# Reordered first quarter, undivided score visits and 13 constant products in an attention and MLP kernel

## Chip, cores and metric

One core of one Trainium2 chip runs the kernel. The metric is device time in microseconds (us). A smaller number is better.

## What is computed

Eight batches of eight heads, 576 queries of 64 elements, with 16 beacon keys ahead of the 576 ordinary ones; then a two-layer MLP over all 4608 tokens:

```python
scores = scale * np.matmul(q, k_all.transpose(0, 1, 3, 2))   # k_all = [beacon_k, k]
scores = np.where(causal, -1000000000.0, scores)              # beacons are always visible
a = np.exp(scores - scores.max(-1, keepdims=True))
a /= a.sum(-1, keepdims=True) + 1e-09
x = np.matmul(a, v_all)          # to [4608 tokens, 512]
h = x @ w_in                     # 512 -> 2048
out = (h * (1.0 / (1.0 + np.exp(-1.702 * h)))) @ w_out        # 2048 -> 512
```

## The kernel before

**Tiles.** A *set* is four heads of one batch, stacked on the 128 partitions, so a batch is two sets (0 and 1 for the first batch, 2 and 3 for the second). Loads of q and k (288 KB each) come through GpSimd's DMA queue, which also converts them to 16 bit. VectorE turns them (`e_turn`, L472) into `qT` and `kT`; a set can be scored once both are turned. The scores of a set are computed in *visits* (the program's chunks, `e_qk`, L509): 512 or 384 columns at a time for four heads, each followed by an exponential on ScalarE (L521) and masks on GpSimd or VectorE. Visits 0 to 15 belong to sets 0 to 3, four to a set; visits 8 to 11 are those of set 2 and visits 12 to 15 those of set 3. A visit is a list of pieces, one for each block of 128 keys; each piece is 2 products for each of 4 heads. `qk_pieces` sorts the pieces by width and, where the last one is wider than 64 columns, cuts 32 columns off it as a piece of its own: the narrow product.

**Values and MLP.** `av s.x.h` (L598) multiplies the exponentials of set s with the values: x = 2 gives the sums, x = 0 and 1 the two halves of the head; h is the half of the queries. Value blocks j = 0 to 4 and the beacon values are loaded separately. `av0.0.1` therefore needs blocks 3 and 4 of the first batch too. `e_norm` (L632) normalises into `xT`. `m1.g.n` (L656) is the first MLP product of token group g (groups 0 and 1 are 256 tokens, later ones 512) for columns n and n+1 of blocks of 128; `tanh` (ScalarE, L671) and `gate` (VectorE, L690) follow. `m2.g.mt.qt` (L702) is the second product for quarter qt of the rows of w2. Every `av`, `m1` and `m2` result stands in one of four PSUM banks (`RING`), which comes free when its norm, gate or eviction has run.

**Order.** `ORDER` gives, by hand, the order of work on every engine; its numbers count the calls of `plan.op`. The planner walks these lists with estimated durations, which decides PSUM banks and how many constant products are put into gaps. Each engine runs its list strictly in order. `Q` is the order in which the planner takes GpSimd's loads to be served, at most 8 of them in flight (`LANES`): load n is issued when load n-8 has landed. GpSimd also makes masks, so a mask listed behind a load waits for that load's turn. SyncE's list holds the beacon-key loads and the stores.

**Constant products.** TensorE has nothing to do until the first keys are turned. The loop at L1380 fills this and later gaps (until 20 us of the planned time) with products of a constant tile, `scrap`, written by VectorE at L327. A gap of n units of 256 columns gets n//4 products in 32 bit and n%4 in 16 bit.

Important names of the diff, in the order's numbering: TensorE 120, 138, 141 are visits 5, 6, 7; 236, 241, 243, 246 visits 8 to 11; 267, 272, 274, 277 visits 12 to 15; 409, 412, 415, 422, 440 visits 16 to 20. GpSimd 49 and 51 are the loads of k and q of set 2, 53 and 55 those of set 3; 25 and 27, 33 and 35, 37 and 39, 41 and 43 are the four column quarters of w1; 17, 19, 21, 23, 29, 31 the beacon values and value blocks 0, 1, 2, 3, 4 of the first batch; 45, 47, 57, 59 are w2; 16 builds the two mask tables. VectorE 235 and 234 turn q and k of set 2, 266 and 265 those of set 3.

Of the kernel before, what the change touches and what calls it, by code (L numbers as in the profile page):

```python
# [14 lines left out]

ORDER = {
    "PE": [
        76, 97, 99, 104, 106, 124, 111, 113, 127, 129, 116, 118, 145, 148, 150, 159, 120, 163, 160, 164, 138, 170,
        131, 141, 167, 173, 176, 236, 136, 152, 134, 157, 179, 241, 155, 182, 197, 243, 200, 203, 206, 246, 209, 212,
        267, 191, 221, 192, 185, 272, 215, 222, 274, 186, 218, 277, 187, 223, 193, 409, 224, 188, 194, 250, 255, 257,  # L20
        281, 253, 412, 227, 228, 229, 415, 288, 286, 262, 260, 291, 284, 293, 422, 230, 321, 311, 313, 309, 299, 303,
        317, 307, 319, 301, 305, 315, 329, 325, 327, 323, 440, 431, 347, 352, 353, 348, 349, 354, 350, 443, 434, 438,
        436, 355, 358, 469, 374, 359, 360, 368, 361, 575, 369, 363, 370, 375, 364, 578, 479, 365, 371, 376, 366, 584,
        482, 377, 484, 486, 603, 380, 516, 494, 605, 381, 382, 383, 518, 608, 488, 510, 514, 490, 498, 492, 504, 500,
        512, 508, 502, 506, 496, 547, 541, 542, 536, 537, 538, 543, 539, 594, 736, 548, 563, 544, 549, 550, 739, 564,
        565, 566, 599, 742, 617, 597, 601, 552, 553, 749, 624, 622, 554, 555, 620, 767, 557, 558, 559, 560, 626, 770,
        758, 569, 570, 571, 646, 572, 656, 636, 654, 796, 763, 761, 652, 644, 630, 632, 640, 638, 642, 628, 648, 634,
# [17 lines left out]
        1546, 1554, 1555, 1556, 1557, 1560, 1561, 1562, 1563,  # L45
    ],
    "ACT": [
        3, 1, 77, 78, 98, 100, 105, 107, 112, 114, 117, 119, 121, 161, 139, 165, 142, 168, 171, 174, 237, 177, 242,
        180, 183, 198, 244, 201, 204, 247, 207, 210, 268, 213, 273, 216, 275, 278, 219, 410, 189, 225, 195, 413, 416,
        424, 423, 231, 322, 312, 314, 300, 310, 318, 304, 308, 320, 306, 316, 302, 330, 326, 328, 324, 441, 351, 444,  # L50
        470, 471, 576, 579, 585, 586, 604, 606, 517, 519, 511, 489, 495, 515, 491, 493, 499, 513, 509, 501, 505, 503,
        507, 497, 609, 540, 737, 740, 743, 751, 750, 768, 771, 627, 647, 657, 637, 655, 797, 653, 633, 631, 639, 641,
        643, 645, 649, 629, 635, 651, 798, 903, 678, 906, 913, 912, 931, 933, 936, 838, 820, 826, 836, 816, 822, 832,
        834, 818, 846, 840, 824, 828, 830, 842, 844, 1064, 867, 1067, 1070, 1077, 1078, 1095, 1098, 1125, 1124, 960,
# [5 lines left out]
        1480, 1476, 1458, 1486, 1484, 1482, 1496, 1460, 1494, 1500, 1502, 1506, 1490, 1510, 1492, 1498, 1508, 1531,  # L60
    ],
    "DVE": [
        73, 75, 74, 101, 103, 102, 79, 87, 82, 80, 81, 125, 109, 110, 126, 108, 130, 128, 146, 147, 151, 149, 162,
        235, 132, 133, 166, 233, 234, 172, 175, 169, 137, 153, 154, 158, 135, 264, 178, 156, 265, 181, 419, 199, 184,
        92, 202, 266, 205, 406, 211, 208, 214, 408, 217, 407, 420, 220, 295, 251, 252, 256, 254, 258, 421, 259, 282,
        466, 283, 289, 287, 263, 261, 290, 285, 292, 294, 467, 468, 296, 427, 297, 428, 429, 335, 336, 298, 339, 581,
        331, 332, 430, 340, 341, 333, 343, 432, 342, 337, 433, 334, 338, 344, 345, 435, 439, 437, 356, 346, 475, 583,
        476, 477, 478, 362, 582, 480, 481, 733, 367, 746, 483, 372, 485, 487, 378, 384, 748, 747, 735, 734, 613, 590,
        520, 521, 591, 532, 533, 534, 592, 793, 528, 524, 535, 529, 525, 526, 530, 593, 527, 531, 595, 596, 522, 523,
        545, 551, 614, 615, 616, 600, 618, 598, 619, 602, 625, 754, 623, 621, 755, 556, 756, 757, 561, 908, 567, 794,  # L70
        759, 795, 760, 573, 764, 762, 802, 910, 803, 909, 1073, 804, 805, 658, 659, 670, 666, 766, 807, 667, 660,
# [12 lines left out]
        1526, 1542, 1547, 1552, 1558, 1564,  # L84
    ],
    "POOL": [
        10, 8, 14, 12, 17, 16, 25, 21, 19, 23, 35, 27, 49, 33, 51, 31, 37, 115, 39, 43, 29, 41, 53, 122, 123, 65, 63,
        140, 61, 45, 144, 55, 143, 67, 388, 47, 239, 386, 390, 69, 238, 57, 59, 245, 240, 249, 392, 400, 404, 269,
        271, 248, 71, 446, 270, 448, 276, 402, 394, 279, 398, 450, 280, 452, 411, 715, 414, 464, 713, 460, 719, 458,
        717, 417, 418, 456, 396, 425, 462, 442, 426, 445, 473, 472, 577, 775, 589, 727, 721, 729, 731, 588, 773, 474,  # L90
        580, 725, 607, 454, 1042, 587, 1040, 723, 777, 779, 611, 610, 738, 612, 741, 744, 745, 753, 789, 781, 752,
        772, 1044, 787, 783, 785, 1046, 769, 791, 800, 799, 1100, 1102, 904, 1050, 1056, 801, 1058, 907, 1048, 914,
        1054, 915, 934, 938, 1104, 939, 916, 937, 1052, 1106, 1108, 1068, 1110, 1072, 1114, 1118, 1071, 1079, 1065,
        1116, 1096, 1112, 1099, 1126, 1080, 1127, 1128, 1144, 1147, 1156, 1154, 1155, 1174, 1179, 1178, 1177,
    ],
    "Q": [
        11, 9, 15, 13, 18, 26, 22, 20, 24, 36, 28, 50, 34, 52, 32, 38, 40, 44, 30, 42, 54, 66, 64, 62, 46, 56, 68,
        389, 48, 387, 391, 70, 58, 60, 393, 401, 405, 72, 447, 449, 403, 395, 399, 451, 453, 716, 465, 714, 461, 720,
        459, 718, 457, 397, 463, 776, 728, 722, 730, 732, 774, 726, 455, 1043, 1041, 724, 778, 780, 790, 782, 1045,
        788, 784, 786, 1047, 792, 1101, 1103, 1051, 1057, 1059, 1049, 1055, 1105, 1053, 1107, 1109, 1111, 1115, 1119,  # L100
        1117, 1113,
    ],
# [141 lines left out]
def kernel(  # L244
# [11 lines left out]
    nc = tc.nc  # L256
# [7 lines left out]
    P = 128  # L264
# [43 lines left out]
    tB = [cst.tile([P, HN, HM], F16, tag=f"tB{i}", name=f"tB{i}") for i in range(3)]  # L308
# [13 lines left out]
        nc.vector.memset(t[:, NK:, :], 0.0)  # L322
    nc.vector.memset(ones, 1.0)
    nc.vector.memset(ones[:, 32:48], 0.0)
    scrap = tB[0][:, 4:6, :].rearrange("p a n -> p (a n)")
    for i, x in enumerate((1.7, -0.6)):
        nc.vector.memset(scrap[:, i::2], x)  # L327
    FIRST, WARM, COLS = 3800, 20000, 256
# [34 lines left out]
    def pieces(s):  # L363
        return list(zip(PIECES, ecol)) if s < EARLY else list(zip(WPIECES, wcol))
# [18 lines left out]
    for s in range(EARLY, NSET):  # L383
        c = 0
        while c < ETOT:
# [3 lines left out]
            w = min(room, ETOT - c)  # L389
# [47 lines left out]
    def e_load_w1(hs, c0, c1):  # L437
        nc.gpsimd.dma_start(
            out=w1t[:, 2 * hs : 2 * hs + 2, c0:c1],
            in_=moe_w_in[2 * P * hs : 2 * P * (hs + 1), c0:c1].rearrange("(p x) n -> p x n", x=2),  # L440
        )
# [17 lines left out]
    def f32(ap):  # L459
        return ap.bitcast(F32)  # L460
# [16 lines left out]
    def qk_pieces(i):  # L477
        got, o = [], 0
        for (s, c0, c1) in CHUNKS[i]:
            for (j, a, e), col in pieces(s):  # L480
                u, v = max(c0, col), min(c1, col + e - a)
                if u < v:
                    got.append((v - u, s, j, a + u - col, o))
                    o += v - u
        got.sort(key=lambda x: -x[0])
        w, s, j, a, o = got[-1]
        if w > 64:
            got[-1:] = [(w - 32, s, j, a, o), (32, s, j, a + w - 32, o + w - 32)]
        return got

# [409 lines left out]
    def pool_load(dur, ns, deps, emit, due=0, pr=0, name=""):  # L900
        i = plan.op("POOL", dur, deps, emit, due=due, pr=pr, name=name)
        i.lands = plan.op("Q", ns, [i], lambda: None, name=name + "q")
        return i.lands
# [34 lines left out]

    def load_w1(c0, c1, due=0):
        return [  # L940
            pool_load(700, 5 * (c1 - c0) // 2, [], lambda hs=hs: e_load_w1(hs, c0, c1), due=due, name="w1")
            for hs in range(HS)
        ]

# [15 lines left out]
    def chunk(i):  # L960
        deps = []
        for s, c0, c1 in CHUNKS[i]:
            if c0 == 0:
                turns(s)
                deps += [avs.get((s - NE, x, h)) for x in range(3) for h in range(2)]
            deps += [turn[(s, 0)], turn[(s, 1)]]
        w = sum(2 * x[0] / 2.4 + 10.5 for x in qk_pieces(i))
        halved = i < len(PAIRED)
        split = halved and PAIRED[i] == "S"
# [98 lines left out]
    def w1_cols(c0, c1):  # L1068
        got = load_w1(c0, c1)
        for nt in range(c0 // P, c1 // P):  # L1070
            w1_of[nt] = got
# [300 lines left out]
    for o in order:  # L1372
        if o.eng == "PE" and o.start < WARM:
            free = [(max([0] + [c.end for c in plan.closers.get(x, ())]), i) for i, x in enumerate(held)]
            since, i = min(free)
            n = int((2.0 if until > FIRST else 1.8) * (o.start - max(until, since + 200)) / COLS)
            if n > 1:
                idle = psu.tile([P, 512], F32, tag=f"u{i}", name=f"u{i}")
                for x in [f32(scrap)] * (n // 4) + [scrap] * (n % 4):
                    nc.tensor.matmul(idle[:, 0:COLS], x[:, 0:P], x[:, 0:COLS], start=True, stop=True)  # L1380
            until = o.end
        if o.eng == "PE" and o.dur and o.ring is not None:
            for x in [o.ring] + [d.ring for d in o.deps if d.ring is not None and not d.dur]:
                if plan.tiles[x] < RING:
                    held[plan.tiles[x]] = x
        o.emit()
# [30 lines left out]
```

## Time and profile before

| | us |
|---|---|
| median of 3 runs | 323.47 |
| lowest and highest | 323.36, 323.74 |
| the profiled execution, its own time | 324.34 |
| its span in the trace | 322.5 |
| TensorE busy in the span | 313.7 (97%) |
| VectorE, ScalarE, GpSimd busy | 247.4, 219.6, 112.8 |
| TensorE clock granted, mean | 0.998 |

The profiled execution took 0.87 us more than the median, and 1.8 us of it lie outside its span. TensorE's share contains the constant products. A busy matmul can also be one that waits for something in its pipeline, so a stretch is best read from start to start: eight `m1` products of 256 columns take 0.98 us from the start of the first to the start of what follows.

### The profile page before, as it was taken

The page shows a single profiled execution, that of the slowest core. Times are in us where ns is not written, and L with a number is a line of the kernel's source. Part 1 is how long each engine was busy: PE and PEld are TensorE (multiplying, and loading weights), DVE is VectorE, ACT ScalarE, POOL GpSimd, SP SyncE. Part 2 cuts the span into 40 slices and gives each one's busy share as a digit, 9 for nine tenths or more (in the row PEclk, how much of TensorE's full clock was granted, in tenths as well). Part 3 has the DMA queues.
Part 4 walks back from the last instruction along what each step waited for, and adds up shares of the span by engine and source line. Part 5 has one row for each costly group of instructions (what it writes and reads, how often), then busy time and mean ns, then how long its engine had stood idle before and what let it go on. Part 6 is the DMA issues. An engine that isn't in the chain of part 4 may idle for free.

```text
span 322.5 us, 10233 instructions
## 1 busy us (share of the span) xinstructions
PE 313.7 (97%) x4466; PEld 231.6 (72%) x4466; DVE 247.4 (77%) x481; ACT 219.6 (68%) x275; POOL 112.8 (35%) x178
## 2 busy tenths in 40 slices
PE   7988999999999999999999999999999999999995
PEld 6666855654786467764778878746788888888884
DVE  3759946898894888876888969888988975684783
ACT  1776776676876777598867685778679786666520
POOL 8668776264226703562083307330420000000000
PEclk9999999999999999999999999999999999999999
DMA  7999999999017971299174807700011000010113
GB/s 118 156 201 191 202 202 188 187 166 124 2 47 120 165 104 35 20 152 119 35 77 84 122 2 62 118 33 2 4 66 67 2 12 25 33 68 34 68 57 108
DMA packets 58222, 28.85 MB, mean 89 GB/s; under 512 B 41280, under 2 KB 53568, under 8 KB 58176
## 3 DMA queue, kind: packets, MB, share of 16 engines
q0 software_dynamic: 47552, 18.49, 48.8%
q1 hardware_dynamic: 10560, 9.69, 9.1%
q8 instruction: 35, 0.57, 0.7%
q14 instruction: 11, 0.09, 0.1%
q10 hardware_dynamic: 64, 0.01, 0.0%
HBM read 37.22 MB, written 9.44 MB: 145 GB/s over the span
## 4 chain that ended last, share of the span: by engine, by line
PE 87%; DMA 6%; ACT 3%; DVE 2%; POOL 1%; issue 1%; DVEq 0%; ACTq 0%; POOLq 0%
PE u L771 31%; PE u L656 23%; PE u L858 11%; PE u L598 9%; PE s L509 8%; PE u L702 4%; DMA qn<-in_q_dram 3%; DMA w<-in_moe_w_in_dram 2%; ACT E L521 1%; ACT L678 1%; DVE kT L472 0%; DVE qT L472 0%; POOL qn L416 0%; ACT g L678 0%; POOL kn L416 0%
## 5 line engine op out<-in xcount | busy, mean ns | idle before, releaser
L521 ACT ACTIVATE E<-s 128x2048 f16<-128x2048 f32 (+3 forms) x59 | 90.7, 1551 | 41.7 <-PE s L509 37.8
L656 PE MATMUL u<-xT,w 128*128 128x256 f16 (+1 forms) x512 | 88.0, 326 | 0.6 <-DMA w<-in_moe_w_in_dram 0.4
L539 POOL TENSOR_SCALAR_AFFINE_SELECT E<-E 128x512 f16<-128x512 f16 (+3 forms) x78 | 48.5, 636 | 89.5 <-ACT E L521 89.5
L656 PEld LDWEIGHTS <-w 128*128 128x128 f16 x512 | 49.0, 98 | 33.6 <-issue 1.4
L678 ACT ACTIVATE g<-u 128x512 f16<-128x512 f32 x80 | 43.3, 600 | 15.6 <-PE u L656 15.0
L771 PEld LDWEIGHTS <-g 128*128 128x128 f16 x512 | 48.5, 98 | 6.9
L787 DVE SCALAR_TENSOR_TENSOR osb<-u,osb 128x512 f32<-128x512 f32 x48 | 32.9, 685 | 23.0 <-PE u L771 18.2
L771 PE MATMUL u<-w,g 128*128 128x256 f16 x384 | 50.2, 273 | 0.0
L771 PEld LDWEIGHTS <-sA 128*128 128x128 f16 x384 | 36.6, 98 | 4.9
L509 PEld LDWEIGHTS <-kT 32*128 32x128 f16 x1376 | 26.2, 92 | 19.0 <-issue 11.3
L886 ACT ACTIVATE g<-u 128x512 f16<-128x512 f32 x48 | 27.0, 602 | 15.0 <-PE u L858 9.1
L771 PE MATMUL u<-tB,sA 128*128 128x256 f16 x256 | 34.2, 273 | 0.0
L509 PE MATMUL s<-qT,kT 32*128 32x32 f16 (+14 forms) x1256 | 31.6, 228 | 1.0 <-DVE kT L472 0.7
L632 DVE TENSOR_TENSOR xT<-u,rz 128x352 f16<-128x352 f32 (+2 forms) x52 | 26.0, 520 | 5.2 <-PE u L598 4.2
L432 POOL DMA_DIRECT2D vb<-in_v_dram x32 | 27.8, 869 | 5.4 <-PE u L598 3.4
L598 PE MATMUL u<-E,vb 128*32 128x352 f16 (+8 forms) x928 | 27.3, 262 | 0.6 <-issue 0.6
L598 PEld LDWEIGHTS <-vb 128*32 128x32 f16 (+1 forms) x928 | 20.0, 96 | 5.3 <-issue 1.8
L472 DVE STREAM_TRANSPOSE qT<-qn 128x576 f32<-128x576 f32 x16 | 19.9, 1243 | 5.0 <-DMA qn<-in_q_dram 4.2
L557 DVE TENSOR_TENSOR zs<-zs,E 128x1344 f16<-128x1344 f16 (+2 forms) x36 | 21.7, 602 | 1.0
L472 DVE STREAM_TRANSPOSE kT<-kn 128x576 f32<-128x576 f32 x16 | 20.1, 1257 | 1.7 <-DMA kn<-in_k_dram 0.6
L858 PEld LDWEIGHTS <-w 128*128 128x128 f16 x192 | 18.7, 98 | 2.2
L858 PE MATMUL u<-xT,w 128*128 128x256 f16 x144 | 20.1, 273 | 0.0
(76 smaller groups left out, 399.5 us busy)
## 6 DMA issues: line engine op xcount, KB each, us to landing
out_dram<-osb SPq DMA_DIRECT2D x36, 256.0 KB, 2.2
qn<-in_q_dram POOLq DMA_DIRECT2D x16, 288.0 KB, 6.4
kn<-in_k_dram POOLq DMA_DIRECT2D x16, 288.0 KB, 6.4
vb<-in_v_dram POOLq DMA_DIRECT2D x24, 128.0 KB, 5.6
w<-in_moe_w_in_dram POOLq DMA_DIRECT2D x8, 256.0 KB, 9.6
w<-in_moe_w_out_dram POOLq DMA_DIRECT2D x4, 512.0 KB, 11.1
vb<-in_v_dram POOLq DMA_DIRECT2D x8, 112.0 KB, 5.8
vb<-in_v_dram POOLq DMA_DIRECT2D x8, 80.0 KB, 5.3
```

What stands on the lines that cost most here:

```text
L432: nc.gpsimd.dma_start(out=t[0 : hi - lo, j, h0:h1, :], in_=v[b, h0:h1, lo:hi, :].rearrange("h n d -> n h d"),)
L472: nc.vector.transpose(out=f32(dst.rearrange("p n e -> p (n e)")).rearrange("p (r t) -> p t r", t=TR), in_=f32(src[:, :]).rearrange("p (t c ...
L509: nc.tensor.matmul(u[:, o : o + w], kT[s % NB2][r : r + 32, j * P : (j + 1) * P, d], qT[s % NB2][r : r + 32, a : a + w, d], start=(d == 0) ...
L521: nc.scalar.activation(out=Es[s][:, h0:h1, c0:c1], in_=sall[(i, p)][:, :, o : o + c1 - c0], func=AFT.Exp, scale=0.125,)
L539: nc.gpsimd.affine_select(out=blk, in_=blk, compare_op=ALU.is_ge, fill=0.0, base=off + (Nb if j == 0 else 0), pattern=[[0, Q], [1, w]], ch ...
L598: nc.tensor.matmul(u[32 * h : 32 * h + 32, a:e], lhs, src[0:kw, h, col : col + e - a], start=first, stop=last, skip_group_check=s >= EARLY ...
L656: nc.tensor.matmul(u[:, o + a - t0 : o + e - t0], w1t[:, kp, nt * P : (nt + 1) * P], xT[:, kp, a % XR : (e - 1) % XR + 1], start=(kp == 0 ...
L678: nc.scalar.activation(out=gts[g][:, n0:n1, 0:w], in_=rings[("m1", g, n0)][:, 0 : n * w].rearrange("p (n w) -> p n w", n=n), func=AFT.Gelu ...
L771: nc.tensor.matmul(u[:, HM * mt : HM * (mt + 1)], lhs[:, n, mt * P : (mt + 1) * P], rhs[:, n, :], start=(n == 0 and mt == 0 and p not in ( ...
L787: nc.vector.scalar_tensor_tensor(out=osbs[(g, dst)][:, :], in0=rings[("p", g, p)][:, :], scalar=scale_of(g), in1=osbs[(g, src)][:, :], op0 ...
L858: nc.tensor.matmul(u[:, HM * n : HM * (n + 1)], lhs[x][:, (2 * i + n) * P : (2 * i + n + 1) * P], rhs[:, x, :], start=fresh and n == 0 and ...
L886: nc.scalar.activation(out=gts[g][:, n : n + 2, HM * h : HM * (h + 1)], in_=rings[src][:, :].rearrange("p (n w) -> p n w", n=2), func=AFT. ...
```

## The change

Four things are changed. (1) A visit of the first sixteen ends with its last piece whole; no narrow product is cut off. (2) `scrap` is twice as wide (1024 elements for 512), and a gap of n units is filled by wider products, in sizes of 8, 4, 2 and 1 units, 13 in all. (3) The planner's duration of a w1 load of 512 columns is 1408 ns for 1280. (4) The orders of TensorE (positions 6 to 147 of 553), ScalarE (13 to 68), VectorE (1 to 127), GpSimd (0 to 98) and its loads (0 to 62) are new; SyncE's is as before, and from those positions on all orders are as before.

```diff
@@ ORDER, the part around visits 5 to 16
     "PE": [
-        76, 97, 99, 104, 106, 124, 111, 113, 127, 129, 116, 118, 145, 148, 150, 159, 120, 163, 160, 164, 138, 170,
-        131, 141, 167, 173, 176, 236, 136, 152, 134, 157, 179, 241, 155, 182, 197, 243, 200, 203, 206, 246, 209, 212,
-        267, 191, 221, 192, 185, 272, 215, 222, 274, 186, 218, 277, 187, 223, 193, 409, 224, 188, 194, 250, 255, 257,
+        76, 97, 99, 104, 106, 124, 127, 111, 113, 116, 118, 129, 145, 148, 120, 150, 159, 163, 138, 164, 160, 131,
+        141, 167, 134, 236, 170, 136, 152, 157, 241, 173, 176, 179, 243, 182, 155, 246, 197, 200, 267, 203, 206, 209,
+        272, 212, 215, 274, 221, 222, 277, 185, 218, 409, 186, 187, 250, 257, 412, 223, 188, 224, 255, 281, 288, 253,
...
     "DVE": [
-        235, 132, 133, 166, 233, 234, 172, 175, 169, 137, 153, 154, 158, 135, 264, 178, 156, 265, 181, 419, 199, 184,
+        233, 132, 234, 162, 133, 135, 169, 166, 137, 264, 153, 406, 154, 158, 172, 175, 178, 266, 156, 265, 181, 184,
...
     "POOL": [
-        10, 8, 14, 12, 17, 16, 25, 21, 19, 23, 35, 27, 49, 33, 51, 31, 37, 115, 39, 43, 29, 41, 53, 122, 123, 65, 63,
-        140, 61, 45, 144, 55, 143, 67, 388, 47, 239, 386, 390, 69, 238, 57, 59, 245, 240, 249, 392, 400, 404, 269,
+        8, 10, 14, 12, 21, 19, 17, 23, 29, 25, 27, 16, 35, 51, 33, 49, 31, 37, 115, 39, 43, 41, 123, 122, 55, 53,
+        140, 388, 143, 386, 144, 45, 47, 57, 238, 63, 392, 240, 67, 65, 61, 59, 269, 390, 245, 248, 71, 69, 270, 239,
...
@@ scrap
-    scrap = tB[0][:, 4:6, :].rearrange("p a n -> p (a n)")
+    scrap = tB[0][:, 4:8, :].rearrange("p a n -> p (a n)")
@@ qk_pieces
-        if w > 64:
+        if w > 64 and i >= 16:
@@ load_w1
-            pool_load(700, 5 * (c1 - c0) // 2, [], lambda hs=hs: e_load_w1(hs, c0, c1), due=due, name="w1")
+            pool_load(700, 11 * (c1 - c0) // 4, [], lambda hs=hs: e_load_w1(hs, c0, c1), due=due, name="w1")
@@ the constant products
-                for x in [f32(scrap)] * (n // 4) + [scrap] * (n % 4):
-                    nc.tensor.matmul(idle[:, 0:COLS], x[:, 0:P], x[:, 0:COLS], start=True, stop=True)
+                for size in (8, 4, 2, 1):
+                    x, w = (f32(scrap), 64 * size) if size > 2 else (scrap, 256 * size)
+                    for _ in range(n // size if size == 8 else n % (2 * size) // size):
+                        nc.tensor.matmul(idle[:, 0:w], x[:, 0:P], x[:, 0:w], start=True, stop=True)
```

TensorE's work from visit 5 to visit 12, by name:

- before: half of m1.0.0, visit 5, three more halves of m1.0.0 and m1.0.2, visit 6, m1.0.6, av0.2.1, visit 7, m1.0.4, m1.0.8, m1.0.10, **visit 8**, av0.1.1, av1.2.1, av0.0.1, av1.1.1, m1.0.12, visit 9, av1.0.1, m1.0.14, m1.1.0, visit 10, m1.1.2, m1.1.4, m1.1.6, visit 11, m1.1.8, m1.1.10, **visit 12**
- after: visit 5, av1.1.0, two halves of m1.0.0 and m1.0.2, visit 6, the other two, av0.2.1, visit 7, m1.0.4, av0.0.1, **visit 8**, m1.0.6, av0.1.1, av1.2.1, av1.1.1, visit 9, m1.0.8, m1.0.10, m1.0.12, visit 10, m1.0.14, av1.0.1, visit 11, m1.1.0, m1.1.2, **visit 12**, m1.1.4, ...

The scores, and the work on them, thus come ahead of MLP products from visit 5 on; the second products of group 0 (191 to 194) and of group 1 are what moves furthest back. Visit 20 (440) is at position 98 of TensorE in both orders. Among the loads, value blocks 0 to 3 of the first batch now precede the first w1 load, q of set 2 precedes k, both loads of set 3 and those of set 4 come directly behind the last w1 load and ahead of w2, and the second batch's values come behind three of the four w2 loads.

## The prediction

> **What bounds the kernel now.** I read the slices first, then TensorE's idle time in the first 100 us, then the chain of waits, then TensorE's timeline where the chain leaves the loads. Two of the page's slices (each is 8 us):
>
> ```profile
> PE   7988999999999999999999999999999999999995
> DMA  7999999999017971299174807700011000010113
> ```
>
> The DMA engines are full for about ten slices, 80 us; TensorE is full from the fifth slice on. TensorE's waits in the first 100 us:
>
> ```profile
> PE u L1380 <- DVE tB L327: 2.0, 1, 2.0
> PE s L509 <- DVE kT L472: 0.7, 1, 0.7
> PE u L598 <- issue: 0.6, 1, 0.6
> PE u L656 <- DMA w<-in_moe_w_in_dram: 0.4, 1, 0.4
> PE u L598 <- POOL E L539: 0.2, 1, 0.2
> ```
>
> All but a few tenths of this lies before 30 us. So the new orders can gain only there; from 30 us to visit 20 at 81.18, TensorE has no hole to fill, and the same work remains. The chain (start, length, what):
>
> ```profile
> 5.20 7.84 DMA w<-in_moe_w_in_dram
> 13.33 11.13 DMA qn<-in_q_dram
> 24.48 1.26 DVE qT L472
> 26.72 0.65 DVE g L690
> 28.04 1.27 DVE kT L472
> 29.99 2.24 PE u L598 x80
> ```
>
> The load of q of set 2 lands at 24.46; its turn, then a gate and the turn of k (landed at 20.5, yet turned last) hold visit 8 until 29.35. TensorE's timeline there, beginning with visit 7:
>
> ```profile
> 24.39 0.72 PE L509 MATMUL s<-qT,kT 32*128 32x208 f16 x32
> 25.04 1.42 PE L656 MATMUL u<-xT,w 128*128 128x256 f16 x10
> 26.91 1.70 PE L656 MATMUL u<-xT,w 128*128 128x256 f16 x14 [0.44 <-DMA w<-in_moe_w_in_dram]
> 29.35 0.64 PE L509 MATMUL s<-qT,kT 32*128 32x288 f16 x24 [0.74 <-DVE kT L472]
> ```
>
> From 25.04 to 29.35 it does 24 products; at 0.98 us for eight that is 2.9 us of 4.3. This is what can be won.
>
> **Method.** TensorE must do the same products before visit 20 in both orders, and its switches between score, value and MLP work number 40 before and 41 after. I therefore compare a moment of the old timeline with the moment of the new one, correct for the products that were moved across it, and ask how much waiting is gone. Durations from start to start: visit of 384 columns 0.47 (36.08 to 36.54), of 512 columns 0.57 (29.35 to 29.92); eight `m1` products 0.98 with a switch, 0.87 without; `av` of 20 products 0.55 (two in 31.05 to 32.16). Visit start to exponential start 0.71 (19.36 to 20.07); the exponential lasts 1.45 or 1.88, and the next visit starts 0.05 later. So visits follow each other in 2.2 us at best, 2.6 behind a wide one.
>
> **Start to visit 5.** Loads of set 0 change places: k is turned first (6.04), q from 7.64, visit 0 at 8.95 for 8.97: nothing. Twice the scrap makes two memsets of 0.28 into about 0.53, so the products begin near 2.53 for 2.03. Slow passes are 0.43 until about 6.46, later ones half that; the products still end near 8.3. `av0.0.0` before visit 3 costs the exponentials 0.25; visit 4 ahead of `av0.1.0` takes back the 0.21 ScalarE waited at 16.97 and the 0.17 at 12.48 has no change. I get visit 5 at 18.3 for 19.36, with 0.66 us of products not yet done: 0.4 gained.
>
> The Trainium skill, "TensorE: Matmul & The Clock Gate", section on what is actually happening, says the activity window is free-running, about 3.4 us long, and only a busy one opens the clock. The row agrees so far as its slow passes end at 6.46, 4.4 us after the first product; by the rule a start 0.5 us later can miss one window in some executions.
>
> **Loads.** The view of each load gives its issue and its time to landing. The landings of before follow each other by about 1.25 us for a w1 load (25.65, 26.90, 28.15), 1.5 for q or k (6.0, 7.6, 9.0, 10.4) and 0.85 for a value block (block 3 at 29.0). All loads up to value block 4 are the same but for value block 3, which now lies ahead of them. Block 4 landed at 24.6; with 0.85 it lands at 25.5, k of set 2 at 25.2, q near 21.4. The keys of set 3 land at 33 in both (31.6 and 37.3 before, so the later of the two is 4 us earlier), and no visit of set 3 waits for them.
>
> **Visits 5 to 8.** Visit 6 waits for visit 5's exponential until 20.5, visit 7 until 22.7 (masks for `av0.2.1` are now ahead of set 3's loads on GpSimd, so its 0.25 wait goes). m1.0.4 ends at 24.15. `av0.0.1` needs block 4: **a new wait of 1.4 us**, until 25.55. Behind it on TensorE stand visit 8 and m1.0.6. Visit 8 needs k's turn, 25.2 + 1.26, so it starts at 26.6. Before, it came at 29.35 with three eights of `m1` products more done (2.6 us) and one `av` pass less (0.55), 2.1 us in all. Gain: 29.35 - 26.6 - 2.1 = **0.6 us**, rounded down. VectorE's gates stand behind that turn, and SyncE's beacon loads, whose memsets move by about 1 us, land long before.
>
> **Visits 8 to 16.** From 26.55 VectorE has gate, z, norm, two gates, norm, two casts, z1, z2, norm, three gates, turn of q, norm, turn of k in a row, 10.6 us nearly without a hole. The four banks come free in that order. I find waits of 0.1, 0.2, 0.05 and 0.05 for banks (m1.0.6 to av1.1.1) and 0.25 before visit 11 for an exponential; 0.3 before visit 14. Each is a difference of two chains that I know to 0.2. Bounds: nothing (the bank is free in time) to 0.95. On GpSimd the masks of set 1 now stand behind k and q of set 4, whose places in flight come free when k and block 4 land (25.2, 25.5); the masks end near 28, before `av1.2.1` at 29. w2, needed at 44, lands earlier than before. I take nothing, since the same orders put two of the five waits within 0.05 of none and the rest within my error; the upper bound is the first rival.
>
> **Narrow products.** Twelve of the sixteen visits have one (the first of each set ends with 48 columns). Eight products each:
>
> ```profile
> 36.08 0.54 PE L509 MATMUL s<-qT,kT 32*128 32x192 f16 x24
> 36.54 2.79 PE L656 MATMUL u<-xT,w 128*128 128x256 f16 x24
> 39.27 0.55 PE L509 MATMUL s<-qT,kT 32*128 32x208 f16 x32
> 39.75 1.92 PE L656 MATMUL u<-xT,w 128*128 128x256 f16 x16
> ```
>
> Both are visits of 384 columns, one in 24 products (0.46 us), one in 32 (0.48). Eight products more cost 0.02. Twelve times that is 0.24; some falls into waits. I take 0.2. No row shows a visit that ends wide: a product of 192 columns lasts 0.248, of 32 columns 0.172, so at worst the exponential starts 0.076 later, 0.9 over twelve visits if each were waited for; four are (5, 6, 10, 13), so the bounds are -0.3 to +0.24. Fewer columns are not streamed, so I stay near the gain.
>
> **Sum.** 0.6 + 0.2 = 0.8 us: span 322.5 to 321.7, the execution 324.34 to 323.5. That execution lies 0.87 over the median; taken from the median, 323.47 - 0.8 = 322.7. The planner's figure for w1 acts only through the orders: nothing. A measurement of this kernel can tell about 0.2%, 0.65 us, from no change.
>
> **Rivals.** *Banks eat it.* If the waits after visit 8 come as I found them, 0.95, the total is 0.8 - 0.95: 323.6, or 323.4 with half of visit 11's hidden. For it: VectorE is 92 to 98% busy from 30 to 40 already. Against: gates wait there for ScalarE, not TensorE for gates. *The loads land late* (the slower side). `av0.0.1` and visit 8 hang on block 4 and k, with nothing behind them on TensorE that may pass. One old w1 load landed 2.15 behind its neighbour (16.8 to 18.95), 0.9 over the usual 1.25. Then k lands at 26.1, visit 8 starts at 27.5, and the 0.6 turns to -0.3; with the bank waits of 0.95 and 0.2 for the narrow products: 1.05 us slower, 324.5. It decides from k at 25.85 on (0.6 above my 25.2 and some tenths). For it: the chain's own load took 11.1 us from issue. Against: fewer loads are late than on time. *The clock opens late.* If the first products stay slow until visit 0, 35 units at 0.213 from 2.53 end at 10.0, 1.05 us late. The wait of 1.4 at `av0.0.1` covers it; if the loads are early it doesn't, and the time is 322.7 + 1.05 = 323.8. The section named above would have it in executions whose window begins in that half microsecond. *The orders do nothing*: TensorE full throughout, 323.3; I count it with the first rival.
>
> **Chances.** Forecast 0.48, of which 0.07 ends within 0.2%; its own range 321.7 (the loads 0.7 early, 1.0 more kept) to 323.1. Banks 0.27, of which 0.01 slower. Late loads 0.21, slower. Clock 0.04, within. So faster 0.41, within 0.07 + 0.26 + 0.04 = 0.37, slower 0.22. The range reaches over the rivals up to 324.3, short of the late loads' full price; below, 321.6.
>
> **What will show it.** Right: visit 8 near 26.6, a wait of TensorE for a value load ahead of it, visit 12 near 37.5 (38.1 with the bank waits), visit 20 near 80.4 for 81.18, 16 products in a visit that had 24 with a narrow end, 24 in one that had 32. Wrong: visit 8 after 27.2, TensorE waiting for gates or norms between 27 and 50 by more than 1 us, visit 20 after 81.2, or a change behind visit 20, where I have none.

## The result and the profile after

| | before | after |
|---|---|---|
| median of 6 runs, us | 323.42 | 322.15 |
| lowest, highest | 323.13, 323.74 | 321.81, 322.63 |
| ratio to before | | 0.996 [0.9947, 0.9973] |
| span of the profiled execution | 322.5 | 320.9 |
| visit 8 starts at | 29.35 | 25.29 |
| visit 12 | 41.60 | 36.31 |
| visit 16 | 53.59 | 46.58 |
| visit 20 | 81.18 | 79.07 |

The change is 1.27 us faster by the medians, 0.4%. Forecast was 0.8. Both profiles are of executions above their kernels' medians (324.34 us for 323.42, and 322.63 for 322.15), so times of one profile set against the other are uncertain by some tenths. The chain that ended last is now almost TensorE alone; in the profile of before its first line read PE 87% and DMA 6%. This is that line of the page after:

```profile
PE 96%; ACT 2%; DVE 1%; issue 0%; ACTq 0%
```

TensorE's waits in the first 100 us of the kernel after, in the same view as before (what waited, for whom, us in total, times, longest):

```profile
PE u L1382 <- DVE tB L327: 2.6, 1, 2.6
PE u L598 <- DVE osb L787: 0.6, 1, 0.6
PE s L509 <- ACT E L521: 0.3, 1, 0.3
```

The waits for w1, for the turn of k, for a mask and on "issue" are all gone. Left is one of 0.3 us for an exponential (0.2 before), and a new one of 0.6 for a join has come. TensorE's timeline after, at three places (start, length, what, count, and in brackets the idle time before it):

```profile
2.59 6.80 PE L1382 MATMUL u<-tB 128*128 128x512 f32 x10 [2.59 <-DVE tB L327]
9.33 0.64 PE L509 MATMUL p<-qT,kT 32*128 32x288 f16 x24
...
23.21 0.53 PE L509 MATMUL s<-qT,kT 32*128 32x208 f16 x24
23.68 1.05 PE L656 MATMUL u<-xT,w 128*128 128x256 f16 x8
24.65 0.68 PE L598 MATMUL u<-E,vb 128*32 128x288 f16 x20
25.29 0.65 PE L509 MATMUL s<-qT,kT 32*128 32x288 f16 x24
...
97.58 0.75 PE L598 MATMUL u<-E,vb 128*32 128x352 f16 x20 [0.57 <-DVE osb L787]
```

First, the constant products last until 9.39 and hold visit 0 until 9.33, although q was turned by 8.3. Second, from visit 7 (23.21) to visit 8 (25.29) there is no hole: the 1.4 us wait for value block 4, which I had forecast, is not there. Third, 0.57 us are lost near 97 us, behind visit 20, where I had expected no change.

### The profile page after: what moved, and what is told of

Read it like the earlier page. It is cut to its first block, busy times and chain, and to the rows that moved or that the text cites. A ratio compares the mean times of both kernels' runs of the same rounds, so it can differ in the third digit from the quotient of the medians.

```text
span 320.9 us, 10025 instructions
## 1 busy us (share of the span) xinstructions
PE 313.5 (98%) x4359; PEld 227.5 (71%) x4359; DVE 247.2 (77%) x481; ACT 219.7 (68%) x275; POOL 112.9 (35%) x178
## 4 chain that ended last, share of the span: by engine, by line
PE 96%; ACT 2%; DVE 1%; issue 0%; ACTq 0%
PE u L771 31%; PE u L656 26%; PE u L858 11%; PE u L598 10%; PE s L509 9%; PE u L702 5%; PE u L1382 3%; PE p L509 1%; ACT E L521 1%; DVE osb L787 0%; ACT L678 0%; DVE tB L327 0%; ACT g L678 0%; DVE kT L322 0%; DVE bkf L319 0%
## 5 line engine op out<-in xcount | busy, mean ns | idle before, releaser
L787 DVE SCALAR_TENSOR_TENSOR osb<-u,osb 128x512 f32<-128x512 f32 x48 | 32.9, 686 | 25.0 <-PE u L771 19.0
L509 PEld LDWEIGHTS <-kT 32*128 32x128 f16 x1280 | 25.1, 92 | 17.8 <-issue 11.1
L509 PE MATMUL s<-qT,kT 32*128 32x32 f16 (+19 forms) x1184 | 31.3, 232 | 0.3 <-ACT E L521 0.3
```

Source lines behind the costliest of these rows:

```text
L509: nc.tensor.matmul(u[:, o : o + w], kT[s % NB2][r : r + 32, j * P : (j + 1) * P, d], qT[s % NB2][r : r + 32, a : a + w, d], start=(d == 0) ...
L787: nc.vector.scalar_tensor_tensor(out=osbs[(g, dst)][:, :], in0=rings[("p", g, p)][:, :], scalar=scale_of(g), in1=osbs[(g, src)][:, :], op0 ...
```

## What the waits on "issue" are

The 0.57 us on "issue" in the kernel before stand here:

```profile
18.68 0.20 PE L598 MATMUL u<-E,vb 128*32 128x48 f16 x3 [0.57 <-issue]
```

The view of busy time by stretch (length, then busy time and count of each engine, clock, DMA share, GB/s) counts the products up to that wait:

```profile
0.00:18.11 18.11, 15.89 (x223) 11.85 (x223) 10.53 (x30) 9.27 (x11) 13.19 (x27) 1.00 1.11 145
```

It comes behind the 223rd product. In the kernels below, every such wait comes behind product 223, 351 or 479, which are 128 apart, or, in two kernels, behind product 990, which is one short of four times 128 further. A product has a weight load, so 128 pairs are 256 instructions. The page of before lists the queue that carries them (packets, MB, share of the DMA engines):

```profile
q8 instruction: 35, 0.57, 0.7%
```

These are packets of 16 KB. With 8932 products and weight loads that is about 255 to a packet; the page of after has 34 for 8718, about 256.

The trace also has the time of each packet, and it ties them to the waits. In the kernel before, a packet of this queue ended at 17.39 us, and TensorE went on at 18.68, 1.3 us later. All 14 waits on "issue" that the traces report, in seven kernels, end in the same way, 1.3 to 1.6 us behind the end of such a packet. So TensorE's program comes in blocks of 256 instructions through the DMA engines, and at a block border TensorE can find the next block missing. Ahead of these 14 waits, with the loads running, the packet started 2.3 to 3.8 us after TensorE had crossed the previous border. Late in the kernel before it is otherwise. From 222 to 317 us, where the page's DMA row reads 0 or 1 up to the last slice, the packet starts between 2.5 us ahead of the border and 0.7 behind it, and no border is waited at. That holds for closely spaced products too: the 128 from 222.87 to 228.15 us took 5.28 us. In that stretch the DMA engines do next to nothing (last columns: clock, DMA share, GB/s; x138 counts every product that overlaps the stretch):

```profile
222.87:228.15 5.28, 5.28 (x138) 4.21 (x130) 5.01 (x11) 4.93 (x4) 0.63 (x1) 1.00 0.01 3
```

So it is the loads that hold a block up. This is read from the traces; no run takes the loads away. The Trainium skill, "Runtime: NRT & Kernel Launch", section on instruction fetch, states the same 16 KB blocks of 256 instructions, and that crossing a border is mostly hidden. The size agrees with the 128 pairs here. The hiding agrees late in the kernel; while the loads run it doesn't, by up to 1.94 us at one border, as the experiments show.

## The experiments

The first four take the change apart: orders alone, undivided visits alone, the old joins behind visit 20, the old early loads.

**Orders alone.** The kernel before with the change's orders on all engines and nothing else:

```diff
     "PE": [
-        76, 97, 99, 104, 106, 124, 111, 113, 127, 129, 116, 118, 145, 148, 150, 159, 120, 163, 160, 164, 138, 170,
+        76, 97, 99, 104, 106, 124, 127, 111, 113, 116, 118, 129, 145, 148, 120, 150, 159, 163, 138, 164, 160, 131,
...
```

> The kernel of before with the new orders alone: narrow products, constant products and the w1 duration stay as before. Theory (the waits ahead of visit 8 go by the orders, the narrow products are worth 0.2 us): 1.1 us faster than before, about 322.3, visit 8 near 25.4, visit 20 near 79.3. Rival (the narrow products are worth more than their 0.02 us a visit, because an exponential starts earlier behind a whole piece): at most 0.7 us faster, 322.7 or more.

Measured: 324.91 us (324.25 to 325.33), ratio to before 1.0044 [1.0032, 1.0057]. It is slower than before, and both theories fail. Two lines of TensorE's timeline show the cause:

```profile
24.86 0.22 PE L509 MATMUL s<-qT,kT 32*128 32x32 f16 x7 [1.11 <-issue]
...
31.06 0.53 PE L509 MATMUL s<-qT,kT 32*128 32x288 f16 x23 [0.97 <-issue]
```

The stretches from 0 to each wait count 351 and 479 products:

```profile
0.00:23.70 23.70, 19.85 (x351) 14.79 (x351) 14.19 (x37) 13.25 (x14) 17.88 (x34) 1.00 1.24 166
0.00:30.10 30.10, 25.13 (x479) 18.74 (x479) 19.65 (x50) 17.94 (x19) 21.92 (x41) 1.00 1.23 175
```

The orders do close the old holes (visit 7 begins at 23.25, as in the kernel after), but TensorE now takes instructions faster than they come: 2.1 us of waiting at two borders. The two waits end 5.9 and 6.2 us after TensorE crossed the previous border. Visit 20 comes at 81.76 for 81.18, and the wait for the join near 100 us, which the new orders bring, costs another 0.55.

**Undivided visits alone.** The kernel before with one line of the change:

```diff
-        if w > 64:
+        if w > 64 and i >= 16:
```

> The kernel of before without the narrow products in visits 0 to 15, all else as before. Theory: 0.2 us faster, 323.2, lost in the waits for loads ahead of visit 8 or just measurable. Rival: 0.6 us or more faster, 322.8 or less.

Measured: 325.47 us (324.15 to 327.3), ratio 1.0066 [1.0042, 1.0091]. 96 products fewer made the kernel 2.2 us slower. The timeline (of the slowest of its executions):

```profile
19.20 0.25 PE L509 MATMUL s<-qT,kT 32*128 32x80 f16 x7 [0.41 <-issue]
...
34.22 0.22 PE L598 MATMUL u<-E,vb 80*32 80x80 f16 x3 [1.62 <-issue]
34.37 3.58 PE L656 MATMUL u<-xT,w 128*128 128x256 f16 x16
...
68.94 0.30 PE L509 MATMUL s<-qT,kT 32*128 32x80 f16 x16 [1.16 <-issue]
```

3.2 us of waits stand behind products 223, 479 and 990. Leaving products out moved the borders to places where the next block had not come. Behind the longest wait the 16 products take 3.5 us from start to start, twice the usual 1.86, because the clock fell (last columns: clock, DMA share, GB/s):

```profile
34.40:37.80 3.40, 3.40 (x19) 0.50 1.43 192
```

So a wait of 1.6 us cost about as much again in this execution. It isn't a rule: behind a longer wait, 1.94 us with the narrow products back (below), the clock stays at 1.00. In the kernel before, too, it is 1.00 from 32 to 40. What the other executions of this kernel waited for isn't in any profile.

**The old joins behind visit 20.** The kernel after, with TensorE's order from position 131 on and VectorE's from 119 on as before:

```diff
     "DVE": [
...
-        367, 372, 378, 485, 483, 487, 384, 748, 746,
+        367, 746, 483, 372, 485, 487, 378, 384, 748,
...
```

> The changed kernel with TensorE's order from position 131 on and VectorE's from 119 on (about 93 us) as in the kernel of before. Theory (the 0.57 us wait at 97 us in the changed kernel comes from the new order of the joins and value passes there): the wait goes and stays gone, 0.6 us faster than the changed kernel, about 321.5. Rival (a bank is short there whatever the order): the wait comes back at another place, 322.1.

Measured: 321.71 us (321.29 to 322.22), ratio to before 0.9949 [0.9938, 0.9961], 0.44 us faster than the change by the medians, though the two intervals overlap. TensorE has no wait between 90 and 100 us in its profile. All six profiled kernels with TensorE's and VectorE's new orders up to there have a wait of 0.55 to 0.57 us for the join; none of the eight with the old ones has it. The change carries a loss of its own.

**The old early loads.** The kernel after, with the first 21 entries of GpSimd's order and the first 20 loads as before:

```diff
     "POOL": [
-        8, 10, 14, 12, 21, 19, 17, 23, 29, 25, 27, 16, 35, 51, 33, 49, 31, 37, 115, 39, 43,
+        10, 8, 14, 12, 17, 16, 25, 21, 19, 23, 35, 27, 49, 33, 51, 31, 37, 115, 39, 43, 29,
...
```

> The changed kernel with the first 21 entries of GpSimd's order and the first 20 loads as before (q ahead of k, mask tables behind the beacon values, value blocks behind the first w1 load, block 3 late). Theory (the order of the early loads made k of set 2 land at 22.6, not chance): the last load of set 2 lands at 24 or later, visit 8 starts at 26 or later, and TensorE waits for a value load ahead of it; 0.7 to 1.5 us slower than the changed kernel, 322.9 to 323.7. Rival (the loads were simply served faster in that execution): set 2 lands before 23, time within 0.3 us of the changed kernel.

Measured: 327.12 us (325.51 to 327.59), ratio 1.0106 [1.0087, 1.0126]. Its profile, of its fastest execution, has the wait that I had forecast for the change itself, only for value block 3 (it lands at 28.2) and not block 4 (23.5):

```profile
28.21 0.31 PE L598 MATMUL u<-E,vb 128*32 128x208 f16 x8 [2.04 <-DMA vb<-in_v_dram]
```

Visit 8 starts at 28.45. The edit also made the planner put three more records of constant products ahead of visit 0, which starts at 9.98 for 9.33; but what TensorE waits for ahead of visit 8 is the value block, not its own late start. Set 2 is complete at 22.9 here, not at 24 or later as the theory had it; what the old order makes late is block 3. The early loads are needed by the new orders. My number for it was too small; what the slower executions lose beyond this one isn't in any profile.

Landings in the profiles of four kernels with the new early loads (the change, orders alone, old joins, and the short start below) and four with the old ones (before, undivided visits alone, this one, and all but the orders below):

| landed at, us | new early loads | old early loads |
|---|---|---|
| first w1 pair complete | 16.4 to 16.7 | 18.5 to 18.9 |
| set 2 complete | 22.6 to 23.4 | 22.9 to 24.5 |
| value blocks 3, 4 | 13.3 to 13.9, 23.1 to 23.9 | 28.2 to 29.0, 23.5 to 24.6 |
| the first 20 loads | 28.2 to 29.0 | 29.5 to 30.3 |

On average the same 20 loads land 1.3 us sooner in the new order, and the execution that I had read was the latest of the four for set 2 and block 4, by 0.3 to 1.5 us.

The next four ask for the constant products, the narrow products in the new orders, the rest of the change without its orders, and a shorter start.

**The old constant products.** The kernel after, with products of 256 columns and a narrower scrap:

```diff
-    scrap = tB[0][:, 4:8, :].rearrange("p a n -> p (a n)")
+    scrap = tB[0][:, 4:6, :].rearrange("p a n -> p (a n)")
...
-                for size in (8, 4, 2, 1):
...
+                for x in [f32(scrap)] * (n // 4) + [scrap] * (n % 4):
+                    nc.tensor.matmul(idle[:, 0:COLS], x[:, 0:P], x[:, 0:COLS], start=True, stop=True)
```

> The changed kernel with the constant products and the scrap tile of before (256 columns each, 8 or 9 more programs' worth of products, scrap half as wide). Theory (TensorE's instructions come in blocks of 128 product-and-weight pairs, and while the loads run a new block takes about 6 us, so every early pair counts): some 17 more pairs put the block borders about 0.8 us earlier; a wait on issue of 0.3 to 1 us appears at product 351, near visit 8; 0.3 to 1.0 us slower than the changed kernel, 322.4 to 323.2. Rival (constant products cost nothing, and the narrower scrap starts them 0.5 us earlier): 0 to 0.5 us faster than the changed kernel, 321.6 to 322.2, no wait on issue.

Measured: 322.22 us (322.04 to 322.65), ratio to before 0.9966 [0.9954, 0.9978], the same as the change. A wait on issue of 0.27 us comes, but behind product 223, at 19.5 us; visit 0 starts at 8.79 for 9.33, and visit 20 at 79.07 in both. The two effects cancel in the profile. The wider constant products gained nothing. (The trace of the kernel after holds 23 records of constant products for 40 here. A product in 32 bit leaves two records, so the 23 are 17 products, not the 13 in the account of the change.)

**Narrow products back.** The kernel after, with the old condition:

```diff
-        if w > 64 and i >= 16:
+        if w > 64:
```

> The changed kernel with the narrow products back. Theory (instruction blocks): 48 more pairs before visit 8, the border at product 351 is reached near 24 us when its block lands at 26; waits on issue of 1.5 to 2.5 us in all at products 351 and 479; 323.7 to 324.7. Rival (a narrow product costs its 0.02 us a visit): 0.2 us slower than the changed kernel, 322.4.

Measured: 325.63 us (325.42 to 325.78), ratio to before 1.0069 [1.0057, 1.0081], 3.5 us slower than the change. The theory had the places, and the waits with 2.4 us in all, but too small a price:

```profile
25.63 0.67 PE L598 MATMUL u<-E,vb 128*32 128x288 f16 x17 [0.43 <-issue]
...
31.83 0.21 PE L509 MATMUL s<-qT,kT 32*128 32x32 f16 x5 [1.94 <-issue]
```

The stretch up to the second wait holds 479 products:

```profile
0.00:31.50 31.50, 26.55 (x479) 16.38 (x479) 21.78 (x53) 18.04 (x19) 23.63 (x43) 1.00 1.22 176
```

Visit 16 starts at 49.61 for 46.58. Of these 3.0 us 2.4 are the two waits.

**All but the orders.** The change with the orders of before:

```diff
     "PE": [
-        76, 97, 99, 104, 106, 124, 127, 111, 113, 116, 118, 129, 145, 148, 120, 150, 159, 163, 138, 164, 160, 131,
+        76, 97, 99, 104, 106, 124, 111, 113, 127, 129, 116, 118, 145, 148, 150, 159, 120, 163, 160, 164, 138, 170,
...
```

> The kernel of before with everything of the change but the orders (no narrow products, fewer and wider constant products, the other w1 duration). Theory (orders and instruction count work together: without the orders TensorE still waits for w1 and the turn of k ahead of visit 8): no faster than 0.5 us than before, 322.9 or more, visit 8 near 28 to 29, and waits on issue only where a border at product 223, 351 or 479 is reached less than 6 us after the one before. Rival (the instructions saved are all of the gain): 322.2.

Measured: 325.52 us (324.2 to 326.78), ratio 1.0066 [1.0041, 1.0091]. Visit 0 starts at 9.84 for 8.97, visit 8 at 28.57 for 29.35, the waits for w1 are there, and issue waits of 0.3 and 1.9 us follow. So neither half of the change is worth anything alone: orders alone cost 1.7 us, the rest alone 2.1, both together gain 1.3.

**A shorter start.** The kernel with the old joins, and fewer constant products ahead of visit 0:

```diff
-            n = int((2.0 if until > FIRST else 1.8) * (o.start - max(until, since + 200)) / COLS)
+            n = int((2.0 if until > FIRST else 1.4) * (o.start - max(until, since + 200)) / COLS)
```

> The changed kernel with the old order of joins and value passes near 97 us, and fewer constant products ahead of visit 0 (the factor 1.8 at 1.4, 27 units for 35). Theory (in executions whose clock opens late the constant products run past the turn of q and hold visit 0 by up to 1.1 us, and from there on TensorE and ScalarE set the pace, not the loads): visit 0 never later than 8.9, 0.3 to 0.6 us faster than the changed kernel with the old joins alone, 321.2 to 321.5. Rival (the loads set the pace up to visit 8, as I had forecast, so an earlier visit 0 is hidden): the same as that kernel, 321.7.

Measured: 321.42 us (321.17 to 321.49), ratio to before 0.9937 [0.9925, 0.9949], 0.73 us faster than the change and 0.29 faster than with the old joins alone, whose interval overlaps with this one. The products now end before q is turned:

```profile
2.60 5.37 PE L1382 MATMUL u<-tB 128*128 128x512 f32 x8 [2.60 <-DVE tB L327]
8.58 0.64 PE L509 MATMUL p<-qT,kT 32*128 32x288 f16 x24 [0.61 <-DVE qT L472]
```

The ten product records ahead of visit 0 took 5.59 us in one profile (old joins) and 6.80 in another (the change): the moment at which the slow passes end differs between executions. Up to visit 8 the loads no longer set the pace, so a late visit 0 is late further on as well: in these two profiles visit 0 starts at 8.62 and 9.33, visit 20 at 78.37 and 79.07. Where the slow passes end early, the long start does no harm: the old joins' profile is of its fastest execution, 321.29 us. The lowest and highest of the short start are 0.32 us apart, those of the old joins 0.93 and of the change 0.82. The long start isn't always wide, though: with the narrow products back it is 0.36.

The last four test the block borders against a price for each product, and two other suspects.

**Narrow products in visits 8 to 15 only**, on the kernel with the short start:

```diff
-        if w > 64 and i >= 16:
+        if w > 64 and i >= 8:
```

> The kernel with the short start and the old joins (e12), with the narrow products back in visits 8 to 15 only. Theory (instruction blocks: what counts is how soon a border is reached behind the one before): border 351 stays near 26, border 479 is reached near 32.1 for 32.7 and its block comes 6 to 6.5 us behind the border before, so at most 0.5 us of issue wait; 0.1 to 0.6 us slower than e12, 321.5 to 322.0. Rival (each narrow product has a price, all twelve visits 3.4): half of it, 1.7 us slower, 323.1.

Measured: 321.62 us (321.46 to 321.77), ratio 0.9946 [0.9934, 0.9958], 0.2 us slower than without them (the intervals overlap) and no wait on issue. The theory holds here. 48 products cost about 0.2 us, 0.033 us a visit.

**Narrow products in visits 0 to 7 only**, on the same kernel:

```diff
-        if w > 64 and i >= 16:
+        if w > 64 and (i >= 16 or i < 8):
```

> e12 with the narrow products back in visits 0 to 7 only. Theory (instruction blocks): border 351 is reached about 0.5 to 1 us sooner and waits some 0.4 us as in the kernel with all narrow products back; border 479 comes late enough and does not wait; 0.3 to 0.8 us slower than e12, 321.7 to 322.2. The two halves together then cost far less than the 3.4 us of the whole. Rival (a price for each product): 1.7 us slower, 323.1.

Measured: 323.99 us (323.54 to 324.54), ratio 1.0016 [1.0007, 1.0025], 2.6 us slower. A price for each product falls: the same number costs 0.2 us late and 2.6 early. But I was wrong about border 479:

```profile
25.63 0.55 PE L598 MATMUL u<-E,vb 128*32 128x288 f16 x15 [0.32 <-issue]
...
31.83 2.25 PE L656 MATMUL u<-xT,w 128*128 128x256 f16 x19 [1.38 <-issue]
```

and the count up to there:

```profile
0.00:31.00 31.00, 26.28 (x479) 16.33 (x479) 21.04 (x53) 19.20 (x20) 23.86 (x44) 1.00 1.22 176
```

From border 351, crossed at 25.63, TensorE runs most of av0.0.1, visit 8, m1.0.6, three more value passes, visit 9 and five products of m1.0.8: 128 products in 4.8 us. The block behind them comes 6.2 us after the border. With the borders of the short start (20.4, 26.4, 32.9) the same passes fall into two blocks and nothing waits. What counts is which products share a block, not how many there are. The three waits on issue in this profile (a third, of 0.15, stands at 19.44) are 1.85 of the 2.6 us, and visit 0 starts 0.25 later; the rest isn't assigned.

**Mask tables early**, on the short start: entry 16 goes back to its old place on GpSimd.

```diff
     "POOL": [
-        8, 10, 14, 12, 21, 19, 17, 23, 29, 25, 27, 16, 35, 51, 33, 49, 31, 37, 115, 39, 43, 41, 123, 122, 55, 53,
+        8, 10, 14, 12, 21, 16, 19, 17, 23, 29, 25, 27, 35, 51, 33, 49, 31, 37, 115, 39, 43, 41, 123, 122, 55, 53,
...
```

> e12 with the mask tables back ahead of the second value load on GpSimd, as early as before (they hold its loads up for 1.1 us near 4.5 us). Theory (the loads now land 1.2 us earlier because the loads' queue is not held up at 4.1 to 5.2 us): the eleventh load lands about 1 us later than 16.6, all twenty at 29.5 or later for 28.9, visit 8 later by 0 to 0.6, time 0 to 0.5 us slower than e12. Rival (eight loads in flight cover the mask tables): landings within 0.3 us of e12's, same time, 321.4.

Measured: 321.32 us (321.21 to 321.58), ratio 0.9938 [0.9926, 0.9951], the same as the short start. The eleventh load lands at 16.7 for 16.6, the twentieth at 28.7 for 28.9. The theory falls; loads in flight cover the tables. Why the new order of the early loads is quicker stays open.

**The old w1 duration** in the kernel after:

```diff
-            pool_load(700, 11 * (c1 - c0) // 4, [], lambda hs=hs: e_load_w1(hs, c0, c1), due=due, name="w1")
+            pool_load(700, 5 * (c1 - c0) // 2, [], lambda hs=hs: e_load_w1(hs, c0, c1), due=due, name="w1")
```

> The changed kernel with the planner's old duration of a w1 load. The orders are fixed, so it changes only which PSUM bank holds which tile and the number of constant products. Theory: within 0.3 us of the changed kernel, 321.9 to 322.5. Rival (the banks that the duration yields matter): 0.5 us or more slower, with new waits of TensorE for gates or norms.

Measured: 322.08 us (321.96 to 322.83), ratio to before 0.9966 [0.9954, 0.9978], the same as the change. Whatever banks it yields don't matter; it acts through the orders found with it, if at all.

## Why the prediction was right, and where it was not

- **What bounds the kernel**: right. The gain lies before 30 us, in the holes ahead of visit 8. I had read the wait on issue as one hole among others and never asked what it was. It was the bound that decides whether the new orders gain or lose.
- **Visits 5 to 8**: the mechanism, visit 8 earlier by more than the products moved behind it, was right; its term was mis-sized. I had 0.6 us; by the same reckoning it is 29.35 - 25.29 - 2.1 = 2.0. TensorE's waits from visit 0 to visit 8 point the same way: those that the views report add up to 2.25 us before and 0.30 after, while visit 0 starts 0.36 later. Two things were wrong in it. The loads: k at 25.2 and block 4 at 25.5, from one execution's landings plus 0.85; they landed at 22.55 and 23.08. So the 1.4 us wait for block 4 did not come. It was one order of loads away: with the old early loads TensorE waited 2.04 us for block 3. And the 0.57 us on issue, which I left where it was, went.
- **Visits 8 to 16**: I took nothing for bank waits, with a bound of 0.95. None came. From visit 8 to visit 20 another 0.1 us was gained (2.11 at visit 20). The rival "banks eat it" did not happen. (With half of visit 11's 0.25 hidden its sum is 323.5, not the 323.4 that I wrote; nothing hangs on it.)
- **Late loads**, the rival on the slower side: not in the change, but its mechanism, TensorE waiting for a value block ahead of visit 8, is shown by the old early loads, which made the kernel 5 us slower than the change.
- **Narrow products**: 0.2 us as a direct price, and the late half alone measured 0.2, 0.033 a visit for the 0.02 that I had read from the timeline. But they were also 96 pairs of instructions in the stretch where blocks come slowly. Putting them back cost 3.5 us. I missed this rival altogether: without these savings the new orders are slower than before.
- **Constant products**: "still end near 8.3" was wrong in the profiled execution (9.39) and right in another (8.18). The "clock opens late" rival was right in what happens and wrong in what covers it: I hid visit 0's delay behind the wait for block 4, which did not exist. In the old joins' profile, where the slow passes end early, my times were good: visits 5, 6 and 7 start at 18.29, 20.44 and 22.51, and I had 18.3, 20.5 and 22.7. A shorter start is 0.29 us faster by the medians.
- **Behind visit 20**: I expected nothing, though TensorE's order differs up to position 147 and visit 20 is at 98; 0.57 us are lost there, and 0.44 came back with the old joins.

The terms together: 2.1 at visit 20, less 0.57, is 1.5 of the 1.6 us between the spans; the medians differ by 1.27.

So the total was nearer than its parts, and that is partly luck. Up to visit 20 I had 0.8 us and the profiles show 2.1; the 0.57 lost behind it, which I had at nothing, hid part of the miss. Of the signs that I had named for being right, the fewer products in a visit came, but the wait for a value load did not, and visits 8, 12 and 20 start 1.2 to 1.3 us earlier than I had said. One of the signs for being wrong came, the change behind visit 20. And that the kernel is faster at all hangs on instructions saved, which I had priced at 0.2 us without seeing what they do to the blocks.

The fastest kernels here are the change with the old joins and the short start, 321.42 us, 0.9937 [0.9925, 0.9949] of before, and the same with the mask tables early, 321.32; the two can't be told apart.

## What to carry to other kernels

A wait on issue in a profile is a reason to count instructions: if it stands a multiple of 128 products behind another, and a packet of the instruction queue ended just before it does, TensorE is waiting for its program, and cutting or moving products ahead of it moves the borders, for better or worse. So a searched order and the number of early instructions should be measured together; here each alone was slower than before. Read landing times from several executions before a sum is built on them, and check that fillers ahead of the first real product end in the slowest of them.

## What the runs showed of the hardware

- TensorE's program comes in blocks of 256 instructions, in packets of 16 KB. Each of the 14 waits on issue ended 1.3 to 1.6 us after such a packet had ended: before 17.39 and 18.68; narrow products back 24.15 and 25.63, 30.27 and 31.83.
- From the previous border to the end of such a wait it was 4.7 to 6.2 us (undivided visits alone 64.28 and 68.94; before 13.85 and 18.68; narrow products back 19.44, 25.63, 31.83). Borders 5.4 to 6.0 us apart were also crossed without a reported wait (20.53, 26.33, 31.77 with narrow products late), so it isn't one fixed figure.
- The loads delay the packet. Ahead of these waits it started 2.3 to 3.8 us after the previous border; in the kernel before from 222 us on, with the DMA engines nearly idle, from 2.5 us ahead of the border to 0.7 behind it.
- A wait of 1.62 us behind a stretch of full work (undivided visits alone) was followed by 3.4 us at a granted clock of 0.50. One of 1.94 us (narrow products back) was followed by a clock of 1.00.
- The constant products' slow stretch ended at different moments in different executions of nearly the same start: the same ten records took 5.59 and 6.80 us.
